# The second stage in 384-token units, with the second column halves of w1 and w2 decoded in place beside the last stage's first blocks

## The chip, the cores and the metric

One core of a Trainium2 chip runs the whole program in one launch. The metric is the device time of that launch in microseconds. TensorE (PE in the profile) multiplies matrices; VectorE (DVE), ScalarE (ACT) and GpSimd (POOL) do the elementwise work; every DMA is issued from the queue of SyncE (SP).

## The reference, cut to what matters

```python
x = attention_with_memory(q, k, v, M_prev, z_prev, beta)   # (4,8,576,64) -> 2304 x 512
h = x @ w_in                                               # 512 -> 2048
x = (h * tanh(softplus(h))) @ w_out                        # 2048 -> 512
a, b = x @ w1, x @ w2                                      # 512 -> 1024 each
out = (a * b @ w3) @ w_out2                                # 1024 -> 1024 -> 512
```

The weights arrive as 64-bit floats, so that each must be decoded on the chip from two 32-bit words. Matrix products are made from a rounded high part and a low part of each operand, three matmuls for one: high by high, high by low, low by high.

## The kernel before

**Stage one** is attention, pair of heads by pair of heads, up to about 257 us. Its result, x transposed, lies in two tiles `xt0` and `xt1` of 1152 tokens each.

**Stage two** (the loop over `u = (g, n)`, L597 to L618 of before) makes 24 units: four quarters `g` of the 2048 inner columns times six chunks `n` of 384 tokens. I number them 6g + n, from 0 to 23. A unit has 48 matmuls of 384 columns for h (`emit_h`, from `xt` and the quarter's weights `wqt`), the activation on ACT, a multiplication `y` on DVE (L436), the split into `gh` (ACT) and `gl` (DVE, L67), and 48 matmuls of 384 columns for x2 (`emit_x2`). The 48 go into four PSUM tiles `psX` out of a ring of three; DVE adds each to `x2` in SBUF (L532), so the fourth tile of a unit needs the first one's add to be over.

Beside the units run **decode steps**, of which one treats 128 rows of a weight matrix: an SP load into `draw`, six DVE instructions (L100, L101, L102, L104, L105, L106), and on POOL an add (L107), a rounding (L64) and a subtraction (L67 or L122). The `draw`, `da` and `de` tiles are rings of two in stage two. Two generators hand out steps of 512 columns: `load_quarter` makes the next quarter's `wqt` (eight steps), and `predecode` writes w1, w2 and w_out2 in two parts to DRAM (24 steps, two stores each), from where they are loaded later. The loop calls `steps(nextq, 2)` and `steps(pre, 1 if n < 4 else 2)` after each unit of the first three quarters.

In the last quarter the generator `fold` runs beside the units: 32 steps of 256 columns decode w3 (here POOL does the add alone), PE transposes them and multiplies them by w_out2, and the product goes through `wo` to DRAM. What is left of it runs on into the last stage. Then `wft` loads that product.

**Stage three** has blocks k of 512 tokens by 128 inner columns: `emit_ab(k)` makes 24 matmuls into two PSUM tiles from `x2h`/`room` (the split of x2, or `x2s` for every other span of tokens) and the weights `w12t`; ACT and DVE make the product and its split into a ring `room` of six; `emit_out(k)` multiplies it by `wft`, 12 matmuls, five blocks later. `w12t` has two slots: columns 0 to 511 of w1 and w2 serve blocks 0 to 3 of a span, columns 512 to 1023 blocks 4 to 7. The slots take the place of `xt0` and `xt1`; both are loaded from DRAM.

The order of instructions on each engine is fixed when the program is built: a scheduler takes the order of the code as priority and places by times that it assumes. Each engine then works strictly in that order.

Of the kernel before, what the change touches and what calls it, by code (L numbers as in the profile page):

```python
# [9 lines left out]
F32 = mybir.dt.float32  # L10
F32R = mybir.dt.float32r
# [10 lines left out]
def fused_kernel(ctx: ExitStack, tc, q, k, v, M_prev, z_prev, beta, w_in, w_out, w1, w2, w3, w_out2, out):  # L22
    nc = tc.nc
    B, H, S, D = q.shape
    NT, DM = out.shape
    FF = w_in.shape[1]
    FF2 = w1.shape[1]
    NP = H // 2
    NB = 5
    KD = DM // 128  # L30
# [10 lines left out]
    dram = ctx.enter_context(tc.tile_pool(name="dram", bufs=1, space=bass.MemoryType.DRAM))  # L41
# [9 lines left out]
    def psX():  # L51
        return bank("X")
# [4 lines left out]
    def f(ap):  # L57
        return ap.bitcast(F32)
# [22 lines left out]
    WN = 512  # L81
# [28 lines left out]
    def words(w, r0, c0):  # L110
        return w[r0:r0 + 128, c0:c0 + dec["w"]].bitcast(I32)

    def split_w(hi, lo, src):
        a, _ = decode(src)
        pool_round(hi, a)
        sub(lo, a, hi, nc.gpsimd)

    def split_to_dram(dst, src):

        a, e = decode(src)  # L120
        pool_round(e.bitcast(F32R), a)
        nc.gpsimd.tensor_tensor(out=a.bitcast(F32R), in0=a, in1=e, op=ALU.subtract)  # L122
        dm(out=dst[0], in_=e)
        dm(out=dst[1], in_=a)
# [9 lines left out]
    nc.vector.memset(half, 0.5)  # L134

    w_dram = dram.tile([2, FF2, DM], F32, name="w_dram")
    w1_dram = dram.tile([2, DM, FF2], F32, name="w1_dram")
    o2_dram = dram.tile([2, FF2, DM], F32, name="o2_dram")
    w2_dram = dram.tile([2, DM, FF2], F32, name="w2_dram")

    def predecode():
        for w, wd in ((w1, w1_dram), (w2, w2_dram), (w_out2, o2_dram)):
            for c in range(w.shape[0] // 128):
                for h in range(w.shape[1] // WN):
                    split_to_dram(wd[:, 128 * c:128 * c + 128, WN * h:WN * h + WN], words(w, 128 * c, WN * h))
                    yield

    xl = {}
# [10 lines left out]
    def load_quarter(g):  # L159
# [24 lines left out]
        out=mask, in_=mask, pattern=[[-1, 512]], compare_op=ALU.is_ge,  # L184
# [272 lines left out]
    pre = predecode()  # L457
# [54 lines left out]
    fk = ExitStack()  # L512
    fpool = [None]

    def emit_x2(u, beside):
        g, n = u
        t = wts[g]
        gg = gt.pop(u)
        c0 = CH * n
        for m in range(KD):  # L520
            o = psX()[:, 0:CH]
            ms = slice(128 * m, 128 * m + 128)
            for kk in range(KQ):
                gh, gl = (x[:, kk % 2] for x in gg[kk // 2])
                mm(o, t[:, 0, KD + kk, ms], gh, kk == 0, False)
                mm(o, t[:, 1, KD + kk, ms], gh, False, False)
                mm(o, t[:, 0, KD + kk, ms], gl, False, kk == KQ - 1)
            d = x2[:, m, c0:c0 + CH]
            if g == 0:
                r = nc.vector.tensor_copy(out=d, in_=o)  # L530
            else:
                r = nc.vector.tensor_tensor(out=d, in0=d, in1=o, op=ALU.add)  # L532
            steps(beside, 1)
        return r.ins
# [44 lines left out]
            held = piece  # L579
            yield  # L580

    def from_dram(t, d, cols):
        for i in range(2):
            dm(out=f(t[:, i]), in_=d[i, :, cols].rearrange("(k p) f -> p k f", p=128))

    def w_slot(s):
        t = xp.tile([128, 2, 2, KD, 512], F32R, tag=f"xs{s}", name="w12t", padded_shape=[128, 2, 2, KD, S])
        for i, wd in enumerate((w1_dram, w2_dram)):
            from_dram(t[:, i], wd, slice(512 * s, 512 * s + 512))
        w1t[s], w2t[s] = t[:, 0], t[:, 1]  # L590

    folding = fold()
    pre0 = iter(())
    nextq = iter(())
    prev = None
    w1t, w2t = [None, None], [None, None]
    for u in [(g, n) for g in range(NQ) for n in range(NCH)]:  # L597
        g, n = u
        last = g == NQ - 1
        if u not in gt:  # L600
            if last and fpool[0] is None:
                steps(nextq, 100)
                steps(pre, 100)
                dk.close()
                fpool[0] = fk.enter_context(tc.tile_pool(name="fp", bufs=1))
                decoder(fk, 3, 2, 256)
            y = emit_h(u, folding if last and n > 0 else iter(()))
        if last and n == 3:
            w_slot(0)
        if prev is not None:  # L610
            with tc.issue_after(emit_x2(prev, folding if last and n > 0 else pre0)):
                split_y(u, y)
        if not last:
            if n == 0:
                nextq = load_quarter(g + 1)
            steps(nextq, 2)
            steps(pre, 1 if n < 4 else 2)
        prev = u  # L618
    NM = FF2 // 128

    steps(folding, 100)
    fk.close()
    late = ctx.enter_context(tc.tile_pool(name="late", bufs=1))
    x2s = late.tile([128, 2, KD, 512], F32R, name="x2s")
    wft = wq.tile([128, 2, NM, DM], F32R, tag="wq0", name="wft")
    for s in range(2):
# [12 lines left out]
    wp3 = ctx.enter_context(tc.tile_pool(name="wp3", bufs=1, side="right"))  # L639
    T = 512  # L640
    RING = 6

    room = w2q[0].tile([128, 2 * RING + KD, T], F32R, tag="wq1", name="room")
    ring = room[:, 0:2 * RING].rearrange("p (r i) t -> p r i t", i=2)

    xs_ = {0: (wp3.tile([128, KD, T], F32R, name="x2h"), room[:, 2 * RING:]), 1: (x2s[:, 0], x2s[:, 1])}

    spans = [(t, min(T, NT - t)) for t in range(0, NT, T)]
    work = [(c, m) for c in range(len(spans)) for m in range(NM)]
# [10 lines left out]
    def emit_ab(k):  # L660
        c, m = work[k]
        n = spans[c][1]
        x = xs_[c % 2]
        pb, pa = (bank(t)[:, 0:n] for t in ("AA", "AF")[m % 2])
        m2 = slice(128 * (m % 4), 128 * (m % 4) + 128)
        for o, w in ((pb, w2t[m // 4]), (pa, w1t[m // 4])):
            for kk in range(KD):
                mm(o, w[:, 0, kk, m2], x[0][:, kk, 0:n], kk == 0, False)
                mm(o, w[:, 0, kk, m2], x[1][:, kk, 0:n], False, False)
                mm(o, w[:, 1, kk, m2], x[0][:, kk, 0:n], False, kk == KD - 1)  # L670
        t = ring[:, k % RING]
# [65 lines left out]
```

## Time and profile before

| | before |
|---|---|
| median of three runs | 1072.71 us (1072.01 to 1073.34) |
| the profiled execution | 1074.7 us |
| its span in the trace | 1072.9 us |
| PE busy | 1032.2 us, 96% |
| DVE, ACT, POOL busy | 667.9, 498.8, 348.1 us |
| mean granted TensorE clock | 0.984 |

A busy PE may run at the lower one of its two clock levels (1.2 instead of 2.4 GHz); the granted clock, 1.00 for the upper level throughout, tells that apart. Times in the trace count from the start of the span.

### The profile page before, as it was taken

What the parts mean: (1) busy time and instruction counts of PE and PEld (TensorE: products, weight loads), DVE (VectorE), ACT (ScalarE), POOL (GpSimd) and SP (SyncE); (2) the same over time, 40 slices, a digit from 0 to 9 for tenths busy, and PEclk for the clock granted to TensorE, in tenths of its full rate; (3) what the DMA queues carried; (4) which work ended last, traced back from release to release, by engine and by line L of the source; (5) the groups of instructions that cost most, each with busy time, mean ns of one, the idle gap of its engine ahead of it and who ended that gap; (6) DMA issues with size and microseconds to landing.
All of it is one profiled execution on the core that took longest, in us unless ns stands there. A gap on an engine that the chain in (4) does not pass through costs nothing.

```text
span 1072.9 us, 15339 instructions
## 1 busy us (share of the span) xinstructions
PE 1032.2 (96%) x5552; PEld 859.0 (80%) x5552; DVE 667.9 (62%) x1484; ACT 498.8 (46%) x1024; POOL 348.1 (32%) x361
## 2 busy tenths in 40 slices
PE   7999999999999998899989999999999999999998
PEld 4565665566899998898989999999768888888897
DVE  5999998754779779988879666667643112121111
ACT  4777777776545554455454554553232122211212
POOL 6767667522345536544455311111100000000000
PEclk9999999999999999899998999999989999999999
DMA  6434344310232422333223256226231010100101
GB/s 149 115 93 111 92 104 107 94 26 18 74 106 99 138 99 100 128 107 137 79 99 118 89 188 226 69 79 229 66 128 69 1 40 1 40 1 0 40 1 59
DMA packets 103675, 94.33 MB, mean 88 GB/s; under 512 B 69552, under 2 KB 75696, under 8 KB 103600
## 3 DMA queue, kind: packets, MB, share of 16 engines
q1 hardware_dynamic: 103600, 93.35, 28.0%
q8 instruction: 44, 0.72, 0.3%
q14 instruction: 31, 0.25, 0.1%
HBM read 71.83 MB, written 21.50 MB: 87 GB/s over the span
## 4 chain that ended last, share of the span: by engine, by line
PE 64%; DVE 17%; POOL 6%; issue 6%; DMA 4%; ACT 2%; SPq 1%; POOLq 0%; DVEq 0%; ACTq 0%
PE psA L61 25%; PE psX L61 20%; PE psF L61 11%; PE psF L378 5%; PE psX L259 3%; POOL da L107 3%; DVE da L104 2%; DVE gl L67 2%; DVE da L100 2%; DVE de L106 2%; DVE da L101 2%; DVE de L105 1%; DVE y L436 1%; DVE da L102 1%; POOL da L122 1%
## 5 line engine op out<-in xcount | busy, mean ns | idle before, releaser
L61 PE MATMUL psX<-gh,wqt 128*128 128x384 f32 x768 | 204.4, 347 | 18.2 <-DVE x L532 17.6
L107 POOL TENSOR_TENSOR da<-da,de 128x512 f32<-128x512 f32 (+1 forms) x88 | 107.4, 1222 | 320.6 <-DVE de L106 272.1
L61 PEld LDWEIGHTS psX<-gh,wqt 128*128 128x128 f32 x768 | 144.1, 195 | 22.1 <-DVE x L532 19.9
L61 PE MATMUL psX<-gl,wqt 128*128 128x384 f32 x384 | 132.9, 348 | 3.0 <-DVE gl L67 2.9
L61 PE MATMUL psA<-xt,wqt 128*128 128x384 f32 x624 | 118.2, 340 | 2.9 <-DVE y L436 2.9
L61 PEld LDWEIGHTS psA<-xt,wqt 128*128 128x128 f32 x624 | 110.4, 191 | 5.4 <-DVE y L436 3.9
L330 ACT ACTIVATE s<-s,acc 128x384 f32<-128x384 f32 (+3 forms) x144 | 84.9, 594 | 35.6 <-DVE acc L325 21.4
L100 DVE TENSOR_SCALAR da<-draw 128x512 int32<-128x512 int32 (+1 forms) x88 | 45.7, 523 | 80.5 <-PE psF L557 26.4
L444 ACT CAST gh<-y 128x768 fp32r<-128x768 f32 x48 | 40.1, 836 | 111.5 <-DVE y L436 69.4
L61 PE MATMUL psX<-wft,room 128*128 128x512 f32 x336 | 82.4, 390 | 0.0
L61 PE MATMUL psA<-x2h,w12t 128*128 128x512 f32 (+1 forms) x288 | 80.0, 354 | 0.0
L61 PEld LDWEIGHTS psX<-gl,wqt 128*128 128x128 f32 x384 | 75.3, 196 | 5.6 <-DVE gl L67 5.0
L325 DVE CUSTOM_DVE_ANT_0 s<-psA,mask 128x512 f32<-128x512 f32 (+2 forms) x144 | 65.0, 477 | 21.7 <-PE psA L61 19.1
L673 ACT COPY bs<-psA 128x512 f32<-128x512 f32 (+1 forms) x40 | 21.8, 546 | 116.5 <-PE psA L61 112.4
L61 PE MATMUL psX<-pt,raw 128*64 128x64 f32 (+4 forms) x576 | 75.0, 328 | 0.0
L61 PE MATMUL psF<-xt,wqt 128*128 128x384 f32 x408 | 74.7, 337 | 0.0
L61 PE MATMUL psA<-kt,qt 64*128 64x384 f32 (+3 forms) x256 | 71.3, 487 | 2.9 <-DVE acc L325 2.4
L61 PEld LDWEIGHTS psX<-wft,room 128*128 128x128 f32 x336 | 62.6, 188 | 12.7
L61 PEld LDWEIGHTS psF<-xt,wqt 128*128 128x128 f32 x408 | 71.9, 190 | 0.1
L380 ACT COPY pt<-psF 128x512 f32<-128x512 f32 (+1 forms) x112 | 58.9, 544 | 27.5 <-PE psF L378 23.6
L674 DVE TENSOR_TENSOR bs<-bs,psA 128x512 f32<-128x512 f32 (+1 forms) x20 | 12.7, 634 | 93.1 <-PE psA L61 92.4
L61 PE MATMUL psA<-x2s,w12t 128*128 128x512 f32 x288 | 67.9, 389 | 0.0
(114 smaller groups left out, 2036.6 us busy)
## 6 DMA issues: line engine op xcount, KB each, us to landing
draw<-in_moe_w_out_dram SPq DMA_DIRECT2D x24, 512.0 KB, 3.5
draw<-in_moe_w_in_dram SPq DMA_DIRECT2D x16, 512.0 KB, 3.9
draw<-in_moe_w_dram SPq DMA_DIRECT2D x16, 512.0 KB, 3.8
draw<-in_moe_w_dram SPq DMA_DIRECT2D x32, 256.0 KB, 3.0
w12t<-w_dram SPq DMA_DIRECT2D x8, 1024.0 KB, 9.0
out_dram<-ob SPq DMA_DIRECT2D x18, 256.0 KB, 2.0
raw<-in_q_dram SPq DMA_DIRECT2D x32, 128.0 KB, 2.7
raw<-in_k_dram SPq DMA_DIRECT2D x32, 128.0 KB, 3.1
```

The costliest lines, as they stand in the source:

```text
L61: nc.tensor.matmul(o, lhsT=l, rhs=r, start=start, stop=stop)
L67: return (eng or nc.vector).tensor_tensor(out=dst, in0=src, in1=f(hi), op=ALU.subtract)
L100: V.tensor_scalar(out=ai, in0=hw, scalar1=0x7FFFFFFF, scalar2=None, op0=ALU.bitwise_and)
L101: V.tensor_scalar(out=a, in0=a, scalar1=2.0 ** -15, scalar2=122879.9921875, op0=ALU.max, op1=ALU.min)
L107: nc.gpsimd.tensor_tensor(out=a, in0=a, in1=e, op=ALU.add)
L259: nc.tensor.transpose(pt[:, x:x + 128], src[:, i].rearrange("p h d -> p (h d)"), ident)
L325: nc.vector.tensor_tensor_reduce(out=s, in0=o, in1=m, op0=ALU.add, op1=ALU.min, scale=-scale, scalar=init, accum_out=a,)
L330: nc.scalar.activation(out=s, in_=s, func=AF.Exp, scale=-1.0, bias=a, accum_out=r)
L378: nc.tensor.transpose(o[:, 128 * x:128 * x + 128], src[:, 128 * jb:128 * jb + 128], ident)
L380: nc.scalar.copy(out=t[:, 0:n], in_=o[:, 0:n])
L444: nc.scalar.copy(out=gh, in_=y[i])
L673: nc.scalar.copy(out=bs, in_=pb)
```

## The change

`predecode` decodes only columns 0 to 511 of w1 and w2, and w_out2 first: 16 steps of 512 columns instead of 24. The loop's counts are made anew: `nextq` gives 2, 2, 1, 1, 1, 1 steps over a quarter, `pre` one step in units 1, 3, 4, 5 of a quarter and in unit 2 of the first two. The second halves are decoded by a new generator `second_half`, 16 steps of 256 columns, whose POOL instructions write straight into slot 1 of `w12t`. It is asked for steps in the last `emit_x2` and in blocks 0 to 3 of stage three; the rest comes before block 4. The decode pool stays open until then, and `x2s`, which takes its room, is allocated after.

```diff
     def predecode():
-        for w, wd in ((w1, w1_dram), (w2, w2_dram), (w_out2, o2_dram)):
+        for w, wd in ((w_out2, o2_dram), (w1, w1_dram), (w2, w2_dram)):
             for c in range(w.shape[0] // 128):
-                for h in range(w.shape[1] // WN):
-                    split_to_dram(wd[:, 128 * c:128 * c + 128, WN * h:WN * h + WN], words(w, 128 * c, WN * h))
+                split_to_dram(wd[:, 128 * c:128 * c + 128, 0:WN], words(w, 128 * c, 0))
+                yield
+
+    def second_half(t):
+        for h in range(2):
+            cs = slice(256 * h, 256 * h + 256)
+            for i, w in enumerate((w1, w2)):
+                for c in range(KD):
+                    split_w(t[:, i, 0, c, cs], t[:, i, 1, c, cs], words(w, 128 * c, WN + 256 * h))
                     yield
...
     def w_slot(s):
         t = xp.tile([128, 2, 2, KD, 512], F32R, tag=f"xs{s}", name="w12t", padded_shape=[128, 2, 2, KD, S])
-        for i, wd in enumerate((w1_dram, w2_dram)):
-            from_dram(t[:, i], wd, slice(512 * s, 512 * s + 512))
+        if s == 0:
+            for i, wd in enumerate((w1_dram, w2_dram)):
+                from_dram(t[:, i], wd)
...
-            steps(nextq, 2)
-            steps(pre, 1 if n < 4 else 2)
+            steps(nextq, 2 if n < 2 else 1)
+            steps(pre, 1 if n in (1, 3, 4, 5) or (g < 2 and n == 2) else 0)
...
     steps(folding, 100)
-    fk.close()
-    late = ctx.enter_context(tc.tile_pool(name="late", bufs=1))
-    x2s = late.tile([128, 2, KD, 512], F32R, name="x2s")
...
-    emit_x2(prev, pre0)
-    w_slot(1)
+    rest = second_half(w_slot(1))
+    emit_x2(prev, rest)
...
     for k, (c, m) in enumerate(work):
+        if k == 4:
+            steps(rest, 100)
+            fk.close()
+            late = ctx.enter_context(tc.tile_pool(name="late", bufs=1))
+            x2s = late.tile([128, 2, KD, 512], F32R, name="x2s")
+            xs_[1] = x2s[:, 0], x2s[:, 1]
         emit_ab(k)
+        if k < 4:
+            steps(rest, 3)
```

What the scheduler makes of it is seen at three places. The first is DVE in the second quarter, from the end of one unit to the adds of the next (`x_3429` is x2). Before, in unit 8 (L532 is the add):

```order
L104 SCALAR_TENSOR_TENSOR da<-draw,da 128x512
L100 TENSOR_SCALAR da<-draw 128x512
L105 TENSOR_SCALAR de<-da 128x512
L101 TENSOR_SCALAR da<-da 128x512
L106 SCALAR_TENSOR_TENSOR de<-draw,de 128x512
L102 TENSOR_SCALAR da<-da 128x512
L104 SCALAR_TENSOR_TENSOR da<-draw,da 128x512
L105 TENSOR_SCALAR de<-da 128x512
L106 SCALAR_TENSOR_TENSOR de<-draw,de 128x512
L100 TENSOR_SCALAR da<-draw 128x512
L101 TENSOR_SCALAR da<-da 128x512
L102 TENSOR_SCALAR da<-da 128x512
```

The next row there is the add. After, in unit 9 (L539 is the add):

```order
L67 TENSOR_TENSOR gl<-y,gh 128x768
L106 SCALAR_TENSOR_TENSOR de<-draw,de 128x512
L105 TENSOR_SCALAR de<-da 128x512
L106 SCALAR_TENSOR_TENSOR de<-draw,de 128x512
L539 TENSOR_TENSOR x_3429<-x_3429,psX 128x384
L100 TENSOR_SCALAR da<-draw 128x512
L443 TENSOR_TENSOR y<-y,psA 128x384 x2
```

Twelve decode instructions stood ahead of the first add, and three stand there now. The second place is POOL from the last step of 512 columns on. Before, to the end of its work:

```order
L107 TENSOR_TENSOR da<-da,de 128x512
L64 TENSOR_SCALAR de<-da 128x512
L122 TENSOR_TENSOR da<-da,de 128x512
L107 TENSOR_TENSOR da<-da,de 128x256 x32
L732 UNCONDITIONAL_BRANCH
```

After, the same place:

```order
L122 TENSOR_TENSOR da<-da,de 128x512
L107 TENSOR_TENSOR da<-da,de 128x256 x33
L64 TENSOR_SCALAR w12t<-da 128x256
L67 TENSOR_TENSOR w12t<-da,w12t 128x256
L107 TENSOR_TENSOR da<-da,de 128x256
L64 TENSOR_SCALAR w12t<-da 128x256
L67 TENSOR_TENSOR w12t<-da,w12t 128x256
```

The 16 new steps all stand behind the fold's 32. The third place is PE behind the fold's last matmul, where the second `psF` tiles of blocks 1 and 3 come first. Before, behind them:

```order
L61 MATMUL psF<-x2h,w12t 128x512
L61 MATMUL psX<-wft,room 128x512 x3
L61 MATMUL psA<-x2h,w12t 128x512
L61 MATMUL psA<-room,w12t 128x512
L61 MATMUL psA<-x2h,w12t 128x512 x2
```

After, the same place:

```order
L61 MATMUL psF<-x2h,w12t 128x512
L61 MATMUL psX<-wft,room 128x512 x27
L61 MATMUL psF<-x2h,w12t 128x512
L61 MATMUL psF<-room,w12t 128x512
L61 MATMUL psF<-x2h,w12t 128x512 x2
```

The output matmuls of blocks 0 to 2 were drawn ahead of block 4, and with them one tile of block 5 (its w1 part). Up to `psA` of block 3 PE's order in the last quarter and the fold is unchanged. Block 8, the first on `x2s`, stands behind 96 matmuls of blocks 4 to 7 and 72 of outputs 0 to 5, counted from the first output.

## Rows read from the trace of the kernel before

**Rows 1.** The page: busy time of each engine.

```profile
PE 1032.2 (96%) x5552; PEld 859.0 (80%) x5552; DVE 667.9 (62%) x1484; ACT 498.8 (46%) x1024; POOL 348.1 (32%) x361
```

**Rows 2.** Stretches: length, busy PE, PEld, DVE, ACT, POOL, granted clock, DMA, GB/s.

```profile
300.00:390.00 90.00, 86.22 (x479) 83.89 (x477) 72.90 (x119) 47.40 (x65) 42.16 (x37) 0.98 0.34 114
390.00:480.00 90.00, 80.45 (x422) 79.39 (x423) 84.98 (x130) 42.01 (x57) 47.16 (x39) 0.92 0.30 103
480.00:570.00 90.00, 80.20 (x435) 78.93 (x435) 74.41 (x122) 44.73 (x62) 44.59 (x36) 0.95 0.31 109
570.00:610.00 40.00, 40.00 (x232) 40.00 (x231) 30.14 (x55) 19.44 (x27) 19.04 (x15) 0.99 0.29 99
...
770.00:796.00 26.00, 21.88 (x87) 16.41 (x86) 12.28 (x34) 4.81 (x11) 2.92 (x4) 0.87 0.28 95
796.00:834.00 38.00, 38.00 (x169) 31.49 (x168) 14.20 (x22) 12.11 (x21) 0.00 (x0) 1.00 0.23 80
```

**Rows 3.** PE's longest wait in total, and two of its seven, in time.

```profile
PE psX L61 <- DVE x L532: 17.6, 7, 6.0
...
409.75 0.80 PE L61 MATMUL psX<-gh,wqt 128*128 128x384 f32 x2 [3.71 <-DVE x L532]
...
564.87 1.01 PE L61 MATMUL psX<-gh,wqt 128*128 128x384 f32 x2 [5.99 <-DVE x L532]
```

**Rows 4.** DVE, then POOL, ahead of the first of these waits, in time.

```profile
403.32 1.50 DVE L100 TENSOR_SCALAR da<-draw 128x512 int32<-128x512 int32 x1 [1.20 <-POOL wqt L67]
404.85 0.72 DVE L101 TENSOR_SCALAR da<-da 128x512 f32<-128x512 f32 x1
405.61 1.37 DVE L102 TENSOR_SCALAR da<-da 128x512 int32<-128x512 int32 x1
407.01 0.69 DVE L104 SCALAR_TENSOR_TENSOR da<-draw,da 128x512 int32<-128x512 int32 x1
407.74 0.43 DVE L105 TENSOR_SCALAR de<-da 128x512 int32<-128x512 int32 x1
408.20 0.69 DVE L106 SCALAR_TENSOR_TENSOR de<-draw,de 128x512 f32<-128x512 uint32 x1
...
409.14 0.55 DVE L532 TENSOR_TENSOR x<-x,psX 128x384 f32<-128x384 f32 x1
...
403.23 1.30 POOL L107 TENSOR_TENSOR da<-da,de 128x512 f32<-128x512 f32 x1
404.62 0.68 POOL L64 TENSOR_SCALAR wqt<-da 128x512 fp32r<-128x512 f32 x1
405.38 1.32 POOL L67 TENSOR_TENSOR wqt<-da,wqt 128x512 fp32r<-128x512 f32 x1
```

**Rows 5.** Timeline: the last of the fold's steps of 256 columns.

```profile
780.63 0.28 DVE L105 TENSOR_SCALAR de<-da 128x256 int32<-128x256 int32 x1
780.95 0.43 DVE L106 SCALAR_TENSOR_TENSOR de<-draw,de 128x256 f32<-128x256 uint32 x1
...
781.54 0.73 POOL L107 TENSOR_TENSOR da<-da,de 128x256 f32<-128x256 f32 x1 [1.77 <-DVE de L106]
```

**Rows 6.** Timeline: PE and DVE around the fold's end and the first output.

```profile
779.56 1.19 PE L61 MATMUL psF<-o,w3h 128*128 128x512 f32 x2 [1.40 <-DVE w3l L67]
...
782.25 1.05 PE L61 MATMUL psF<-o,w3h 128*128 128x512 f32 x2
...
786.93 0.63 PE L61 MATMUL psF<-o,w3h 128*128 128x512 f32 x2
...
787.30 0.43 DVE L67 TENSOR_TENSOR w3l<-psF,w3h 128x256 fp32r<-128x256 f32 x1 [1.00 <-ACT w3h L559]
...
795.53 0.84 PE L61 MATMUL psX<-wft,room 128*128 128x512 f32 x3
...
796.03 0.69 DVE L67 TENSOR_TENSOR room<-bs,room 128x512 fp32r<-128x512 f32 x1 [0.69 <-ACT room L675]
```

**Rows 7.** The chain that ended last: one block's 24 matmuls in stage three.

```profile
809.29 5.44 PE psA L61 x24
```

More of the change, by code (lines that the diff above doesn't have):

```diff
@@ L136, in fused_kernel @@
     w_dram = dram.tile([2, FF2, DM], F32, name="w_dram")
-    w1_dram = dram.tile([2, DM, FF2], F32, name="w1_dram")
+    w1_dram = dram.tile([2, DM, WN], F32, name="w1_dram")
     o2_dram = dram.tile([2, FF2, DM], F32, name="o2_dram")
-    w2_dram = dram.tile([2, DM, FF2], F32, name="w2_dram")
+    w2_dram = dram.tile([2, DM, WN], F32, name="w2_dram")
     def predecode():
-        for w, wd in ((w1, w1_dram), (w2, w2_dram), (w_out2, o2_dram)):
+        for w, wd in ((w_out2, o2_dram), (w1, w1_dram), (w2, w2_dram)):
             for c in range(w.shape[0] // 128):
-                for h in range(w.shape[1] // WN):
-                    split_to_dram(wd[:, 128 * c:128 * c + 128, WN * h:WN * h + WN], words(w, 128 * c, WN * h))
+                split_to_dram(wd[:, 128 * c:128 * c + 128, 0:WN], words(w, 128 * c, 0))
[6 more added lines that the diff above has]
+                    split_w(t[:, i, 0, c, cs], t[:, i, 1, c, cs], words(w, 128 * c, WN + 256 * h))
                     yield
@@ L580, in fold, with from_dram @@
             yield
-    def from_dram(t, d, cols):
+    def from_dram(t, d):
         for i in range(2):
-            dm(out=f(t[:, i]), in_=d[i, :, cols].rearrange("(k p) f -> p k f", p=128))
+            dm(out=f(t[:, i]), in_=d[i].rearrange("(k p) f -> p k f", p=128))
     def w_slot(s):
         t = xp.tile([128, 2, 2, KD, 512], F32R, tag=f"xs{s}", name="w12t", padded_shape=[128, 2, 2, KD, S])
-        for i, wd in enumerate((w1_dram, w2_dram)):
-            from_dram(t[:, i], wd, slice(512 * s, 512 * s + 512))
+        if s == 0:
+            for i, wd in enumerate((w1_dram, w2_dram)):
+                from_dram(t[:, i], wd)
         w1t[s], w2t[s] = t[:, 0], t[:, 1]
+        return t
     folding = fold()
@@ L644, in fused_kernel @@
     ring = room[:, 0:2 * RING].rearrange("p (r i) t -> p r i t", i=2)
-    xs_ = {0: (wp3.tile([128, KD, T], F32R, name="x2h"), room[:, 2 * RING:]), 1: (x2s[:, 0], x2s[:, 1])}
+    xs_ = {0: (wp3.tile([128, KD, T], F32R, name="x2h"), room[:, 2 * RING:])}
     spans = [(t, min(T, NT - t)) for t in range(0, NT, T)]
```

## The prediction

> **What bounds the kernel now.** I read the page's busy times first: PE is busy 96% of the span [rows 1], so a change can win only where PE stands still or runs at its lower clock. The table by stretches says where that is [rows 2]. From 300 to 610 us, the body of stage two, PE stands still for 3.8, 9.5, 9.8 and 0 us in the four stretches; the granted clock, 0.98, 0.92, 0.95 and 0.99, takes a further 1.8, 7.2, 4.5 and 0.4 us off its speed (a hundredth less is a hundredth of the stretch). Together 37.0 us, of which 31.0 lie between 390 and 570. From 796 to 834, in the last stage, PE is busy throughout at the full clock and POOL does nothing. The waits say why stage two loses: PE's longest wait is the fourth x2 tile's for the add of the first, 17.6 us in seven waits [rows 3]. The timeline ahead of one of them shows the add at 409.14 behind decode instructions: from 403.32 to 408.89 DVE works off one step, and only then one more instruction and the add [rows 4]. So in this stretch DVE's queue, not PE, sets the pace, and each wait of about 2 us or more is followed by a few us of PE at the lower clock: behind the fold's wait at 779.56 two matmuls of 512 columns take 1.05 us where they take 0.63 later [rows 6].
>
> The same rows price a step. While POOL works on its three instructions (403.23 to 406.70), DVE gets three of its own through, each ending about 0.3 us behind the end of one of POOL's: L100 at 404.82 behind 404.53, L101 at 405.57 behind 405.30, L102 at 406.98 behind 406.70. The other three then take 0.69, 0.43 and 0.69 us with POOL idle. The add, which reads PSUM, is not held up like this.
>
> **Stage two, part by part.** I count, in the order of DVE, the steps that end between the last adds of neighbouring units. Before, units 1 to 16 have 2 2 2 2 2, then 4 3 3 3 2 3 2 2 4, then 2 2: 40. After, they have 2 2 2 2 1, then 2 2 2 2 2 2 3 4 2, then 2 1: 33. The middle nine are about the stretch from 390 to 570 (the add at 409.14 is unit 6's first). The other seven units, all of two steps, lost 37.0 - 31.0 = 6.0 us, 0.86 a unit. At that rate the nine would lose 7.7 without their eight steps beyond two; they lost 31.0, so those eight cost 23.3 us, 2.9 each. After the change fourteen units have two steps or more (14 x 0.86 = 12.0) and three steps are beyond two, in units 12 and 13 (3 x 2.9 = 8.7); the two units of one step I put at nothing. That leaves 20.7 of 37.0: **16 us saved**. Ends: by the plain mean, 37.0/40 a step, the seven fewer save 6.5; the most is all 37. I stay at 16, nearest to the stretch where the steps in excess are taken away; what speaks for more is that only three decode instructions stand ahead of the adds in units 8 to 11, where ten or more stood. Units 17 and later have a full PE already, so a step fewer there is worth nothing; that PE is the cover, and 0 it stays. The two stores a step, sixteen fewer, and the four loads of slot 1, 1 MB each, are off SP's queue; they hid beside PE, and I take nothing for them.
>
> **Last stage.** PE's order up to block 3 is the same, so the fold's end stays as it is, earlier by what stage two saves; for the sum I keep the old times. The new steps cannot start early: on POOL they stand behind the fold's 32 adds, the last at 781.54 [rows 5], and on DVE the first step's last two instructions stand behind the fold's last low part, 787.30 to 787.73 [rows 6]. They add 0.28 and 0.43 us [rows 5], so POOL's first new add starts at about 788.6.
>
> What a step of 256 columns with three POOL instructions costs no row shows, since the fold has only the add. From below: POOL alone, the add's 0.73 [rows 5] and by the ratio 0.73/1.30 = 0.56 of 0.68 and 1.32 [rows 4], 0.38 and 0.74, with 0.1 us between them 2.1 us. From above: DVE and POOL wholly one behind the other, 3 x 0.28 + 0.28 + 2 x 0.43 = 2.0 and 1.85, 3.8 us. Between them: the step at 403.32, 5.57 us, scaled by 0.56 (POOL) to 0.65 (L105 at 0.28/0.43), 3.1 to 3.6. I take 3.1, since a fourth DVE instruction can pass before POOL's next add.
>
> Fifteen steps at 3.1 and the last one's 2.1 on POOL end at 788.6 + 46.5 + 2.1 = 837.2. In between stand ten DVE instructions of blocks 1 to 5, 0.69 us each [rows 6]; half of them I let POOL cover, 3.5 us. The last draws stand behind the second half of wft on SP, 2 MB: 2 us. So the decode ends at about 842.7. Behind it is the split for `x2s`, which waits until the pool is free, one ACT and one DVE instruction ahead of PE: 1.5 us, 844.2.
>
> When does PE want it? It starts outputs at 795.53 [rows 6], and has 96 + 72 matmuls ahead of block 8, at 5.44/24 = 0.227 us [rows 7] 38.1 us, so at 833.6. In that order it waits 10.6 us in all, piece by piece, since k = 4 to 7 take the tiles as POOL hands them over; queued behind a waiting matmul on PE are the outputs of blocks 4 and 5, too, and nothing else of PE's can be drawn forward. Behind a wait PE's clock is low, as at the fold's end, where 0.87 over 26 us costs 3.4 us [rows 2]; half of it I add, 1.7, since most of such a stretch falls into waiting here. **12 us given back.** The ends: a cycle of 2.1 us ends the decode at 788.6 + 31.5 + 2.1 + 7 = 829, and nothing is lost but the 1.5 to 2 us of `x2s`; 3.8 us ends it, with `x2s`, at 854.5, 21 us late, 24 with the clock.
>
> **Sum.** The profiled execution has 1074.7 us, of which 1.8 lie outside the span of 1072.9; less 16, plus 12, it is 1070.7. The median of the runs is 2.0 lower, 1072.71, so 1068.7; I say **1068.5 us**. A measurement of this kernel can tell about 0.2%, 2.1 us, from no change: faster is below 1070.6, slower above 1074.9.
>
> **Rivals.** (1) *The decode hides, and stage two gives more.* With a cycle near 2.1 us and stage two down to PE's pace: 25 saved (between 16 and 37), 2 given back, 1049.7. For it speaks that DVE is busy only 14.2 of 38 us from 796 to 834 and POOL not at all [rows 2]; against it, the pairs in rows 4. (2) *Slower: the new chain binds.* DVE and POOL take turns on every instruction of the 16 steps, 3.8 us each: 24 given back, 16 saved, 1080.7. It decides from where the chain is 14.3 us late (16 with the clock), at a cycle of (847.9 - 1.5 - 5.5 - 2.1 - 788.6)/15 = 3.3 us, just above mine. For it: L100, L101 and L102 all end behind a POOL instruction, and two of the three are more than twice as long as L105. Against it: one of DVE's instructions passes per POOL instruction without making that longer than 1.32 us.
>
> The Trainium skill has a rule for this, in "SBUF — State Buffer", section "Who interferes with whom": one port pair is shared by VectorE and GpSimd as an exclusive lock, held for a whole instruction, by VectorE instructions with two SBUF inputs or in a two-port mode. The trace agrees in kind: L101 ends 0.27 us behind POOL's L64, and the PSUM-reading add keeps its 0.55 us beside POOL's add. By a strict reading the rival's 3.8 us holds and the time is its 1080.7; by the measured step it is mine.
>
> (3) *Stage two hardly gains*, 6.5 us, since the wait for y and gl behind the same steps remains, and the chain costs 12: 1078.2.
>
> **How the numbers follow.** Mine 0.42, its own range 1060 to 1077, as its terms may be off by some 8; rival 1 0.25, rival 2 0.20, rival 3 0.13. Faster: rival 1 and 0.30 of mine, 0.55. Same: 0.09 of mine and 0.05 of rivals 2 and 3, 0.14. Slower: the rest, 0.31. The range of eight in ten leaves out half of rival 1 beyond 1049.7 and the worst of rival 2: 1050 to 1083.
>
> **What would show it.** PE's total wait for L539 adds falls from 17.6 to some 8 us, the rest of it in units 12 and 13, with the granted clock of the middle stretch up from 0.92. POOL, empty after 782 before, works for 48 to 57 us past the fold's end; PE waits some 10 us for POOL's `w12t` in that time, and its granted clock there falls below 1.00. If PE waits for POOL under 3 us, rival 1 holds; over 18, rival 2; if the L539 waits stay above 14 us, rival 3. I am wrong altogether if the fold's end itself moves.

## The result, and the profile after

The changed kernel takes **1061.89 us** (1060.50 to 1063.80) against 1073.03 us for the kernel before, run beside it: a ratio of 0.990, 95% interval 0.988 to 0.992. The prediction was 1068.5 us, in a range of 1050 to 1083. The direction was right, the size was not: 11 us faster, not 4.

The profiled execution took 1060.5 us, its span is 1058.4 us. It is the fastest of its kernel's four, and that of the kernel before, 1074.7 us, lies above its kernel's median: the traces differ by some 14 us where the medians differ by 11. PE's busy line falls by 10.2 us, DVE's by 6.5 [rows 1]:

```profile
PE 1022.0 (97%) x5552; PEld 850.4 (80%) x5552; DVE 661.4 (62%) x1532; ACT 499.4 (47%) x1024; POOL 350.4 (33%) x385
```

The stretches of stage two, then two of the last stage; the columns are those of [rows 2]:

```profile
300.00:390.00 90.00, 87.21 (x498) 85.93 (x498) 71.86 (x124) 51.46 (x70) 43.74 (x34) 1.00 0.28 94
390.00:480.00 90.00, 90.00 (x521) 90.00 (x520) 66.36 (x123) 51.20 (x71) 36.38 (x35) 1.00 0.27 90
480.00:570.00 90.00, 81.25 (x455) 79.97 (x454) 73.48 (x118) 44.27 (x61) 44.29 (x36) 0.98 0.27 95
570.00:590.00 20.00, 20.00 (x117) 20.00 (x116) 8.34 (x21) 11.72 (x17) 1.49 (x2) 1.00 0.09 27
762.00:790.00 28.00, 25.90 (x108) 21.00 (x107) 22.77 (x53) 3.69 (x7) 15.87 (x24) 0.94 0.70 241
790.00:822.00 32.00, 25.09 (x101) 19.66 (x100) 28.44 (x57) 8.25 (x15) 16.58 (x25) 0.95 0.14 45
```

From 390 to 480 us PE stands still for none of the time, at the full clock, where it lost 9.5 us and 0.92 of its clock before [rows 2]. From 300 to 390 it idles 2.8 us, from 480 to 570 8.75, with 1.8 us of clock (0.02 of 90): stage two still loses 13.3 us of its 37.0. In the last two stretches DVE is busy for 51.2 of 60 us and POOL for 32.5.

PE's longest wait in stage two, that for the add (L539 now, L532 before [rows 3]): total, times, longest.

```profile
PE psX L61 <- DVE x L539: 8.7, 4, 3.8
```

Two of the four, the first and the last, in time:

```profile
503.25 0.62 PE L61 MATMUL psX<-gh,wqt 128*128 128x384 f32 x2 [3.79 <-DVE x L539]
...
560.60 0.62 PE L61 MATMUL psX<-gh,wqt 128*128 128x384 f32 x2 [2.46 <-DVE x L539]
```

They are in units 12 to 15, 3.79, 1.29, 1.20 and 2.46 us. The other 2.7 us are unit 1's, at 310 (for gl) and 317.5 (for y). Units 2 to 11 show no wait.

To see where the time went I cut the program at the first matmul that stage three makes behind the fold, block 1's second tile. Before:

```profile
789.01 0.39 PE L61 MATMUL psF<-x2h,w12t 128*128 128x512 f32 x1
```

After, with the first matmul on `x2s`, block 8's:

```profile
762.45 0.39 PE L61 MATMUL psF<-x2h,w12t 128*128 128x512 f32 x1
...
819.20 1.19 PE L61 MATMUL psA<-x2s,w12t 128*128 128x512 f32 x4 [2.38 <-ACT bs L679]
```

Up to the cut 26.6 us are saved. From it to the end of the span it took 1072.9 - 789.0 = 283.9 us, and takes 1058.4 - 762.45 = 295.9: **12.0 us given back**.

### The profile page after: what moved, and what is told of

Same layout as the page of the kernel before. It is cut to its first block, busy times and chain, and to the rows that moved or that the text cites. A ratio compares the mean times of both kernels' runs of the same rounds, so it can differ in the third digit from the quotient of the medians.

```text
span 1058.4 us, 15388 instructions
## 1 busy us (share of the span) xinstructions
PE 1022.0 (97%) x5552; PEld 850.4 (80%) x5552; DVE 661.4 (62%) x1532; ACT 499.4 (47%) x1024; POOL 350.4 (33%) x385
## 4 chain that ended last, share of the span: by engine, by line
PE 66%; DVE 17%; POOL 7%; DMA 4%; issue 3%; ACT 2%; SPq 1%; POOLq 0%; DVEq 0%; ACTq 0%
PE psA L61 25%; PE psX L61 24%; PE psF L61 10%; PE psF L385 5%; PE psX L266 3%; POOL da L107 3%; DVE da L104 2%; DVE da L100 2%; DVE de L106 2%; DVE da L101 2%; DVE y L443 2%; DVE da L102 2%; DMA draw<-in_moe_w_dram 2%; DVE de L105 2%; DVE gl L67 1%
## 5 line engine op out<-in xcount | busy, mean ns | idle before, releaser
L61 PE MATMUL psX<-gh,wqt 128*128 128x384 f32 x768 | 197.3, 336 | 8.9 <-DVE x L539 8.7
L61 PEld LDWEIGHTS psX<-gh,wqt 128*128 128x128 f32 x768 | 138.8, 188 | 12.0 <-DVE x L539 10.0
L61 PE MATMUL psX<-gl,wqt 128*128 128x384 f32 x384 | 128.4, 336 | 0.9 <-DVE gl L67 0.9
L100 DVE TENSOR_SCALAR da<-draw 128x512 int32<-128x512 int32 (+1 forms) x96 | 43.2, 454 | 94.9 <-PE psF L564 28.6
L61 PEld LDWEIGHTS psX<-gl,wqt 128*128 128x128 f32 x384 | 72.2, 188 | 2.1 <-DVE gl L67 1.5
L385 PE MATMUL psF<-ident,s 128*128 128x128 f32 x400 | 65.4, 282 | 1.2 <-ACT pt L387 1.2
```

Source lines behind the costliest of these rows:

```text
L61: nc.tensor.matmul(o, lhsT=l, rhs=r, start=start, stop=stop)
L100: V.tensor_scalar(out=ai, in0=hw, scalar1=0x7FFFFFFF, scalar2=None, op0=ALU.bitwise_and)
L385: nc.tensor.transpose(o[:, 128 * x:128 * x + 128], src[:, 128 * jb:128 * jb + 128], ident)
```

## Experiments

**The two halves apart.** `e1_no_second` keeps the new stage two and leaves out the decode of the second halves: slot 1 is filled from DRAM, from the first halves; `e4_chain_alone` keeps the old stage two and adds the new decode.

`e1_no_second`, against the changed kernel:

```diff
-        if s == 0:
-            for i, wd in enumerate((w1_dram, w2_dram)):
-                from_dram(t[:, i], wd)
+        for i, wd in enumerate((w1_dram, w2_dram)):
+            from_dram(t[:, i], wd)
...
-    rest = second_half(w_slot(1))
+    rest = iter(())
     emit_x2(prev, rest)
+    w_slot(1)
```

`e4_chain_alone`, against the kernel before (`second_half`, `w_slot` and `x2s` as in the change):

```diff
+    rest = second_half(w_slot(1))
+    emit_x2(prev, rest)
...
+        if k < 4:
+            steps(rest, 3)
```

> The changed kernel with its stage two as it is, but without the decode of the second halves: slot 1 of the weights is loaded from DRAM as before, from the first halves, so that decode is the part of the computation that is left out. It shows what stage two saves by itself. Theory (stage two saves about 26 us, by the fold's end at 762.45 instead of 789.01, and the decode chain in the last stage gives about 12 back): 1047 to 1051 us, and PE waits for nothing but the fold between 762 and 820. Rival (the chain costs little by itself, and the last stage is longer for another reason, such as PE's new order of outputs): 1056 to 1062 us.

> The kernel before with its whole stage two (24 steps of predecode, old order and counts) and the changed last stage on top: slot 1 is decoded in place, and the second halves in DRAM stay unused. It shows the last stage's part by itself. Theory: the chain gives back 12 us, 1083 to 1088. Rival (the chain costs only because stage two now ends earlier): 1073 to 1078.

Measured: `e1_no_second` 1048.12 us, ratio 0.977 (0.975 to 0.978), 25 us below the kernel before. `e4_chain_alone` 1087.25 us, ratio 1.013 (1.011 to 1.015), 14 above it. The sum, -25 + 14 = -11, is what the change measures, so the halves add up. The cut says the same: in `e1_no_second` it stands at 762.06 and 283.9 us follow, as before the change; in `e4_chain_alone` it stands at 788.13 and 297.9 follow. What PE waits for in `e4_chain_alone` from 780 on:

```profile
PE psX L61 <- ACT room L682: 4.1, 1, 4.1
PE psA L61 <- ACT bs L680: 2.4, 1, 2.4
PE psF L61 <- DVE bs L681: 2.1, 1, 2.1
```

The same three waits stand in the changed kernel's tail (4.2, 2.4 and 2.1 us); `e1_no_second` has the last kind alone, 0.8 us.

**The number of steps or their place.** The change made the steps fewer and put them elsewhere. `e2_spread` leaves the kernel before its 24 steps of `predecode` and spreads the counts; `e3_old_counts` gives the changed kernel, with its 16, the old counts back.

`e2_spread`, against the kernel before:

```diff
-            steps(nextq, 2)
-            steps(pre, 1 if n < 4 else 2)
+            steps(nextq, 2 if n < 2 else 1)
+            steps(pre, 1 if n < 2 else (2 if n == 3 or n == 5 else 1))
```

`e3_old_counts`, against the changed kernel:

```diff
-            steps(nextq, 2 if n < 2 else 1)
-            steps(pre, 1 if n in (1, 3, 4, 5) or (g < 2 and n == 2) else 0)
+            steps(nextq, 2)
+            steps(pre, 1 if n < 4 else 2)
```

> The kernel before with all its 24 steps of predecode, only the counts of the loop are spread: nextq 2, 2, 1, 1, 1, 1 and pre 1, 1, 1, 2, 1, 2 over a quarter. Theory A (the number of steps in a unit beyond two costs, by DVE's total load): the same 40 steps, so no more than 5 us from before, 1068 to 1075. Theory B (what costs is decode instructions bunched ahead of the x2 adds, and the spread alone undoes that): 1050 to 1060.

> The changed kernel with the counts of before in the loop (nextq 2 a unit, pre 1 or 2): the eight steps fewer stay, the spread is undone, and the steps crowd in quarters 0 and 1. Theory A (load): steps beyond two remain in the first two quarters, about six of them, and quarter 2 has a full PE: 1062 to 1068. Theory B (bunching): the stalls come back in full, 1070 to 1076.

Measured: `e2_spread` 1073.06 us, ratio 0.999 (0.998 to 1.001); `e3_old_counts` 1078.4 us, ratio 1.005 (1.003 to 1.006). In `e3_old_counts` DVE's order has 2 2 2 2 2 4 3 3 3 3 0 2 3 1 steps in units 1 to 14 and none in 15 and 16, and PE's longest wait and the stretch from 390 to 480 us look like the kernel before [rows 2, 3] and not like the changed one:

```profile
PE psX L61 <- DVE x L539: 16.5, 6, 5.2
```

```profile
390.00:480.00 90.00, 79.01 (x429) 77.93 (x430) 85.29 (x131) 42.23 (x59) 47.15 (x39) 0.94 0.31 106
```

So with eight steps fewer, but crowded, stage two keeps most of its loss; the cut comes at 780.11, 17.7 us later than with the same steps spread. `e2_spread` shows the other side: its order has three steps in units 8, 11, 15 and 17 and two in the others from 1 to 18, and it loses some 21 us from 300 to 610, not 37. Two steps a unit are not free there: units 2, 3, 6, 7, 12 and 13, with two each, wait 2.1, 2.2, 1.3, 0.7, 1.4 and 3.7 us. The last of these:

```profile
533.75 0.61 PE L61 MATMUL psX<-gh,wqt 128*128 128x384 f32 x2 [3.72 <-DVE x L532]
```

What it gains it loses again behind 610 us. Its steps reach into units 17 and 18; from 610 to 640 PE stands still for 4.7 us (0.9 before) and its clock is 0.89 (1.00 before), and from 740 to 788 it loses 7 us more than before, wait and clock together. The cut comes at 788.14, 0.9 us earlier than before. Its stretches from 570 on, PE nearly full in the first and not in the second:

```profile
570.00:610.00 40.00, 39.63 (x227) 38.99 (x226) 29.68 (x59) 21.52 (x29) 16.67 (x15) 1.00 0.33 108
610.00:640.00 30.00, 25.28 (x131) 24.32 (x130) 21.93 (x39) 11.29 (x19) 12.79 (x11) 0.89 0.64 218
```

Spread alone and fewer steps alone each gained nothing; the change has both.

**Fewer still, and half the chain.** `e5_fewer_still` is `e1_no_second` with the decode of w2's first half left out too (four steps fewer; w1's first half stands in for it); `e6_half_chain` decodes w1's second half in stage two (four steps more) and leaves only w2's to the last stage.

`e5_fewer_still`, against `e1_no_second`:

```diff
-        for w, wd in ((w_out2, o2_dram), (w1, w1_dram), (w2, w2_dram)):
+        for w, wd in ((w_out2, o2_dram), (w1, w1_dram)):
...
-            steps(pre, 1 if n in (1, 3, 4, 5) or (g < 2 and n == 2) else 0)
+            steps(pre, 1 if n in (1, 3, 5) or (g == 2 and n == 4) else 0)
```

`e6_half_chain`, against the changed kernel:

```diff
+        for w, wd, c0 in ((w_out2, o2_dram, 0), (w1, w1_dram, 0), (w2, w2_dram, 0), (w1, w1b_dram, WN)):
...
-            for i, w in enumerate((w1, w2)):
+            for i, w in ((1, w2),):
...
+            steps(pre, 1)
```

> The kernel of e1_no_second with four more steps taken out of stage two: w2's first half is not decoded either, and both weights' slots are loaded from w1's first half, so that the decode of w2 is left out. In DVE's order units 1 to 17 now have 2 2 2 1 0, 2 2 3 3 1 0, 2 2 3 3 0 0 steps, four beyond two. Theory (units of two steps lose nothing behind a light unit; only crowded ones lose, some 3 us a step beyond two): stage two loses as much as in e1_no_second, whose waits these would be, only elsewhere: 1045 to 1050 us. Rival (each step costs by DVE's total load, some 3 us): 1034 to 1040 us.

> The changed kernel with w1's second half decoded in stage two again (four more steps of 512 columns, one pre step after every unit), so that only w2's eight steps of 256 columns are left for the last stage. Theory (crowding; units 1 to 17 have 2 2 3 2 1, 2 2 3 2 2 2, 3 2 3 2 2 1): stage two loses 0 to 5 us more than in the changed kernel, and the decode chain, half as long, ends ahead of PE's need, so that 8 to 12 us are won: 1050 to 1057 us. Rival (load: four steps at 2.9 us): 1060 to 1065 us.

Measured: `e5_fewer_still` 1062.65 us, ratio 0.990 (0.988 to 0.991), 14.5 us **slower** than `e1_no_second`, which has four steps more. Its order has 2 2 2 1 0 2 2 3 3 1 0 2 2 3 3 in units 1 to 15, gaps and pairs of threes, and waits again in the stretch that was full:

```profile
390.00:480.00 90.00, 84.47 (x479) 83.83 (x478) 69.93 (x116) 47.74 (x65) 38.81 (x33) 0.98 0.25 83
```

Its total wait for L539 adds is 13.6 us. Unit 3, with two steps, waits 2.9 us there. A price by the number of steps, in all or in a unit, does not fit this run. `e6_half_chain` took 1068.48 us, ratio 0.995 (0.994 to 0.997). From its cut, 778.44, 286.8 us follow: half the chain gives back 2.9 us, not half of 12. The four steps more cost 16 us of stage two, much more than was expected of them; its order has a three in units 3, 8, 12 and 14 and one step in 17.

**The chain in the last stage.** `e7_own_ring` starts the second halves earlier, in buffers of their own (128 columns, one `draw`, two `da` and `de`); `e8_round_on_act` moves the chain's rounding from POOL to ACT.

`e7_own_ring`, against the changed kernel:

```diff
-                decoder(fk, 3, 2, 256)
+                decoder(fk, 2, 2, 256)
+                own_ring.update(pool=fk.enter_context(tc.tile_pool(name="dec2", bufs=1)), raw=1, n=2, w=128)
...
+        if last and n == 5:
+            rest = second_half(w_slot(1))
```

`e8_round_on_act`, against the changed kernel:

```diff
-                    split_w(t[:, i, 0, c, cs], t[:, i, 1, c, cs], words(w, 128 * c, WN + 256 * h))
+                    a, _ = decode(words(w, 128 * c, WN + 256 * h))
+                    nc.scalar.copy(out=t[:, i, 0, c, cs], in_=a)
+                    sub(t[:, i, 1, c, cs], a, t[:, i, 0, c, cs], nc.gpsimd)
```

> The changed kernel with the second halves decoded out of rings of their own (128 columns a step, 32 steps, w2 ahead of w1; the fold's draw ring is two instead of three) and asked for right after the last unit's h, so that they no longer stand behind the fold's 32 adds on POOL. Theory (the 12 us are given back because the chain starts only when the fold is over): most of the chain lies beside the fold, 1048 to 1055 us. Rival (DVE has no room beside the fold, so that the fold's end moves out instead): 1060 to 1068 us.

> The changed kernel with the rounding of the second halves on ACT instead of POOL: POOL has two instructions a step, 0.41 us less. Theory (DVE and POOL, by turns, set the chain's pace of some 3.2 us a step): 0.3 to 0.5 us a step, so 4 to 8 us less: 1054 to 1058 us. Rival (the loads of draw or DVE alone set the pace): 1060 to 1063 us.

Measured: `e7_own_ring` 1103.66 us, ratio 1.028 (1.026 to 1.029), far outside what was expected. PE waits 26.6 us for POOL's `w12t`, 0.3 us in the changed kernel, and DVE for loads:

```profile
DVE da L100 <- DMA draw<-in_moe_w_dram: 65.5, 31, 4.1
```

Of these 31 waits 27 are the chain's, with its one `draw`, and four the fold's, whose ring has one `draw` less here; the cut moves out too, by 12.2 us to 774.67. The run changes both rings at once. It doesn't tell whether an earlier start in two `draw` buffers would pay; that was not tried. `e8_round_on_act` took 1062.52 us, ratio 0.989 (0.987 to 0.992), no change. POOL has an instruction of 0.41 us less a step, but waits 0.5 us for ACT in its place, and the last step ends at 815.62 us where it ended at 815.93:

```profile
810.28 0.74 POOL L107 TENSOR_TENSOR da<-da,de 128x256 f32<-128x256 f32 x1 [0.69 <-DVE de L106]
811.54 1.02 POOL L67 TENSOR_TENSOR w12t<-da,w12t 128x256 fp32r<-128x256 f32 x1 [0.52 <-ACT w12t L153]
```

So POOL's share of a step is no shorter, and the run doesn't tell which engine sets the chain's pace.

**Crowding moved about.** Left was what the changed kernel still loses in units 12 to 15, where its order has 3 4 2 2 steps. Two lines of counts move the crowding: `e9_second_quarter` has one three, in unit 7, and a last step in unit 17; `e10_third_quarter` has 3 3 2 2 1 from unit 12 on.

Both against the changed kernel, `e9_second_quarter` first:

```diff
-            steps(pre, 1 if n in (1, 3, 4, 5) or (g < 2 and n == 2) else 0)
+            steps(pre, (0,0,1,1,1,1)[n] if g ==1 else (0,1,1,1,1,1)[n])
```

```diff
-            steps(pre, 1 if n in (1, 3, 4, 5) or (g < 2 and n == 2) else 0)
+            steps(pre, 1 if n in ((1, 2, 3, 4, 5) if g < 2 else (2, 3, 4, 5)) else 0)
```

> The changed kernel with one other line of counts: predecode gives a step in units 2, 3, 4, 5 of the second quarter and in units 1 to 5 of the first and the third (a step in unit 1 of the second quarter goes to unit 2 of the third). Same steps in all, same output; DVE's order has 2 steps in each of units 1 to 16 but unit 5 and 11 (1) and unit 7 (3), and one in unit 17; the changed kernel has 3 and 4 in units 12 and 13 and none beyond 16. Theory (crowding: what is lost hangs on steps beyond two in a unit): the changed kernel's waits at 503 to 561 us (8.7 us with their lower clock some 10) nearly go, one three-step unit costs 2 to 3, and the fold's end comes 5 to 9 us earlier than 762.4: 1053 to 1057 us. Rival (the loss belongs to the end of the third quarter, where the first steps of the last quarter's weights and the last of predecode meet, whatever the count): the waits there stay, 1060 to 1063. A second rival is that the step in unit 17 shifts the fold's start, as in e2_spread, by 3 to 5 us: 1058 to 1060.

> The changed kernel with predecode giving a step in units 2, 3, 4, 5 of the third quarter where it gave 1, 3, 4, 5. Same steps in all, same output; DVE's order has 3 and 3 steps in units 12 and 13 (3 and 4 before), 2 in 14 and 15, 1 in 16. Theory (each step beyond two costs some 3 us): two steps beyond two where there were three, so 3 us off, 1058 to 1060 us, with the waits at 503 to 561 us down from 8.7 to some 6. Rival (the place, not the count): no change, 1060 to 1063.

Measured: 1062.38 us (ratio 0.990, 0.989 to 0.991) and 1062.01 us (0.990, 0.988 to 0.993). By the times alone my theory had fallen, since both stayed with the rival of the place. The trace of `e9_second_quarter` says otherwise: the stretch that lost 10.6 us is full, and a new wait has come at its end.

```profile
480.00:570.00 90.00, 90.00 (x521) 90.00 (x521) 63.83 (x113) 55.19 (x76) 38.86 (x35) 1.00 0.23 79
570.00:590.00 20.00, 16.00 (x90) 15.68 (x89) 9.78 (x23) 9.49 (x13) 4.67 (x4) 0.95 0.23 79
590.00:620.00 30.00, 30.00 (x158) 29.07 (x157) 20.67 (x53) 12.49 (x19) 4.47 (x6) 0.92 0.55 190
```

The timeline ahead of that wait tells why:

```profile
580.61 1.29 POOL L122 TENSOR_TENSOR da<-da,de 128x512 fp32r<-128x512 f32 x1
...
581.93 0.32 SPq L124 DMA_DIRECT2D w_dram<-da  x1
...
583.99 1.28 SPq L94 DMA_DIRECT2D draw<-in_moe_w_dram  x3
...
587.90 0.29 DVE L100 TENSOR_SCALAR da<-draw 128x256 int32<-128x256 int32 x1 [9.23 <-issue]
588.23 0.29 DVE L101 TENSOR_SCALAR da<-da 128x256 f32<-128x256 f32 x1
588.44 0.55 DVE L539 TENSOR_TENSOR x<-x,psX 128x384 f32<-128x384 f32 x1
...
589.04 1.01 PE L61 MATMUL psX<-gh,wqt 128*128 128x384 f32 x2 [4.00 <-DVE x L539]
```

The add at 588.44 stands behind the fold's first two instructions (256 columns). Their `draw` lies in the room of the old decode pool. POOL ends at 581.90, the store of the last step's low part is issued, 2.1 us later the fold's load, 3.9 us after that DVE goes on, having stood idle for 9.23 us. That the room is free only with that store is my reading; the trace shows the order and names no releaser. `e10_third_quarter` has the same wait in unit 16, where its last step stands, beside 4.7 us left in units 12 and 13:

```profile
576.60 0.29 DVE L100 TENSOR_SCALAR da<-draw 128x256 int32<-128x256 int32 x1 [10.06 <-issue]
...
577.74 0.77 PE L61 MATMUL psX<-gh,wqt 128*128 128x384 f32 x2 [3.08 <-DVE x L539]
```

So each of my two tables bought one loss with the other. Three earlier runs have this wait as well: `e3_old_counts` (2.4 us, in unit 14), `e5_fewer_still` (4.9) and `e6_half_chain` (2.9). Unit 14 isn't late, so a late unit isn't the condition. In all five DVE ends the last step of 512 columns behind the first add of a unit, 5 to 10 us ahead of the time when the next unit's add could run; in the changed kernel it ends at unit 15's first add (560.1 us), and unit 16's, at 573.4, keeps nobody waiting. It is the place of the second rival, by another mechanism: the fold's first product isn't later than in the changed kernel (606.58 for 607.12 us), PE waits inside the unit.

**Neither.** If that is so, a table with two steps in every unit and none after unit 15 should gain. The loop has no place for it, but stage one has: there, in the changed kernel, PE is busy for all of 180 to 260 us and DVE for 51.6 of these 80.

`e11_two_a_unit`, against the changed kernel; `e12_one_late` has 14 in place of 15, and one step more in the third quarter:

```diff
-        if 2 <= p < 12:
+        if 2 <= p < 15:
             steps(background, 1)
...
+            steps(pre, (0, 1, 1, 1, 1, 1, 0, 1, 1, 1, 1, 0, 0, 1, 1, 0, 0, 0)[6 * g + n])
```

> The changed kernel with three of its steps of predecode taken into stage one, which asks for a background step in pairs 12, 13 and 14 too, and the counts of the loop made to suit. Same steps in all, same output. DVE's order has two steps in every unit from 1 to 15 (one in 5), none beyond, so neither a third step in a unit nor a last step beside the change of the decode pool. Theory after e9 and e10 (a unit of two steps costs nothing; a third costs 2 to 3 us; and steps after unit 15 delay the change of pools, behind whose first load DVE holds back x2's add, 3 to 4 us and as much again at the lower clock): what stage two loses falls from 13 to about 3 us (the waits at 310 and 317 stay), 9 to 10 us off less 0 to 3 for the steps in stage one, where PE is busy throughout and DVE for 60%: 1052 to 1056 us. Rival (the work has to be done somewhere, and PE pays the same for it wherever it stands, as e9 and e10 look if only their times are read): 1060 to 1063.

> As e11_two_a_unit, with pairs 12 and 13 alone, so that one step more is left for the loop: DVE's order is the same up to unit 15, and has one step in unit 16. Same steps in all, same output. It tells the change of pools apart. Theory: the add in unit 16 or 17 waits behind the first instruction of the fold's first step, 3 to 4 us, with 1 to 3.5 us at the lower clock behind it: 4 to 7 us slower than e11_two_a_unit, 1057 to 1062. Rival (a single step in a unit hides): within 1.5 us of e11_two_a_unit.

Measured: `e11_two_a_unit` **1052.33 us** (1049.30 to 1052.77), ratio 0.980 (0.979 to 0.981), inside what was expected, and better than both kernels. Its stage two is full but for the first stretch:

```profile
300.00:390.00 90.00, 86.85 (x496) 85.26 (x495) 72.30 (x125) 51.05 (x70) 43.60 (x34) 1.00 0.28 95
...
480.00:570.00 90.00, 90.00 (x521) 90.00 (x520) 62.01 (x119) 52.16 (x73) 35.22 (x31) 1.00 0.22 73
570.00:590.00 20.00, 20.00 (x119) 19.97 (x118) 10.01 (x26) 10.89 (x16) 0.89 (x2) 1.00 0.01 2
```

It loses 3.2 us from 300 to 590, 2.7 of them in the waits of unit 1. Those stand 1.5 us later than in the changed kernel (319.0 for 317.5), the most that the three steps can have cost in stage one. The cut comes at 751.18, 11.3 us earlier: 13.3 - 3.2 - 1.5 = 8.6 of it are stage two's, and some 1.8 are the lower clock of the changed kernel's fold (0.92 from 740 to 762 us), which this profiled execution, 3 us below the median of its five, doesn't show; 0.9 stays open. `e12_one_late` took 1054.65 us, ratio 0.983 (0.981 to 0.984), 2.3 us more than `e11_two_a_unit`: one late step costs neither 4 to 7 us nor nothing. Its one wait of the new kind has the shape of that in `e9_second_quarter`:

```profile
566.12 0.29 DVE L100 TENSOR_SCALAR da<-draw 128x256 int32<-128x256 int32 x1 [6.81 <-DMA draw<-in_moe_w_dram]
...
569.01 0.55 DVE L539 TENSOR_TENSOR x<-x,psX 128x384 f32<-128x384 f32 x1
...
569.61 0.61 PE L61 MATMUL psX<-gh,wqt 128*128 128x384 f32 x2 [1.92 <-DVE x L539]
```

Here the last step makes weights that stay in SBUF, so no store stands ahead of the change of pools: the fold's load goes out at 562.55 us, as POOL's last instruction ends at 562.53. The clock stays at 1.00. The mechanism holds, its price is smaller than I said.

## Why the prediction was wrong in size

- **What bounds the kernel** was right: DVE's order in front of the x2 adds. `e3_old_counts` and `e5_fewer_still` show that fewer steps alone win nothing; what counts is their place. What I took for a sign of it was too simple: I read that ten or more decode instructions stood ahead of the adds of units 8 to 11 before (twelve, ten, nine and five did), and in the changed kernel twelve stand ahead of unit 6's first add, 8.5 us of work, without a wait, while twelve in unit 12, 10.7 us of work, cost 3.79 us. I also counted one step too many after: unit 16 has none, so units 1 to 16 have 32 steps, not 33; only the low end of the range of savings hangs on it.
- **The failed step is the price by the number of steps in a unit, above all the 0.86 us for every unit of two**, 12.0 of the 20.7 us that I left to stage two. I took it from seven units outside the middle, and spread their 6.0 us over them. Nine of the fourteen units that I charged, 2 to 4 and 6 to 11, have two steps each and lose nothing in the changed kernel: 7.7 us charged for 0, and the whole sum was 20.7 for a measured 13.3. Unit 1 loses 2.7 us at 310 and 317.5; every run has two steps in it, so whether they are the cause stays open. Two steps are not free in themselves either: in `e2_spread` and `e5_fewer_still` units with two wait, in `e11_two_a_unit` units 2 to 15, with two in all but unit 5, lose 0.3 us. What counts is where a step's instructions stand on DVE against `gl`, `y` and the adds; a rule that gives the wait from the order no run here shows.
- **The excess**: three steps at 2.9 us, 8.7, in units 12 and 13. Measured 8.7 us of waits and 1.8 of clock, in units 12 to 15. That the size came out is luck: units 12 and 13 wait 5.1 us, and the other 3.7 stand in units 14 and 15, which have two steps. The price isn't one of a step. The one three in `e9_second_quarter` cost 2.7 us of waits in units 7 to 10, the three in unit 9 of the kernel before none, and the end of the decode has a price of its own, as `e9_second_quarter` and `e12_one_late` show.
- **The fold**: the cut moved by 26.6 us, of which stage two's body explains 37.0 - 13.3 = 23.7. The fold itself, from its first product to the cut, takes 155.3 us for 156.8, so 1.5 us lie in it, and 1.4 us are left open.
- **The last stage** came out as worked out: 12.0 us given back for 12 in the traces, 14 by the times in `e4_chain_alone`. The chain on POOL ran from 761.94 to 815.93 us, 54.0 us; I had 788.6 to 842.7, 54.1. One of its cycles near the end, up to the next:

```profile
806.73 0.74 POOL L107 TENSOR_TENSOR da<-da,de 128x256 f32<-128x256 f32 x1 [1.15 <-DVE de L106]
807.56 0.41 POOL L64 TENSOR_SCALAR w12t<-da 128x256 fp32r<-128x256 f32 x1
808.04 0.74 POOL L67 TENSOR_TENSOR w12t<-da,w12t 128x256 fp32r<-128x256 f32 x1
809.93 0.74 POOL L107 TENSOR_TENSOR da<-da,de 128x256 f32<-128x256 f32 x1 [1.15 <-DVE de L106]
```

  A cycle is 3.2 us for the predicted 3.1. DVE in the same time:

```profile
806.89 0.73 DVE L101 TENSOR_SCALAR da<-da 128x256 f32<-128x256 f32 x1
807.65 0.45 DVE L102 TENSOR_SCALAR da<-da 128x256 int32<-128x256 int32 x1
808.14 0.92 DVE L104 SCALAR_TENSOR_TENSOR da<-draw,da 128x256 int32<-128x256 int32 x1
809.10 0.29 DVE L105 TENSOR_SCALAR de<-da 128x256 int32<-128x256 int32 x1
809.42 0.42 DVE L106 SCALAR_TENSOR_TENSOR de<-draw,de 128x256 f32<-128x256 uint32 x1
```

  L101, L102 and L104 each end 0.1 to 0.3 us behind one of POOL's three; L105 and L106 follow with POOL idle, and the next add waits for them. The Trainium skill ("SBUF — State Buffer", section "Who interferes with whom") has VectorE instructions with two SBUF inputs or in a two-port mode and GpSimd's exclude each other on a shared port pair. The trace agrees in kind: L105 and L106 are held too where they meet an instruction of POOL (0.70 us at 795.32 and 0.86 at 777.97, for 0.29 and 0.42 here). Even so the step isn't the 3.8 us of rival 2: in this cycle the instructions held under POOL's three add only the 0.28 us by which the last of them, L104, ends behind POOL.
- **What PE waits for in the last stage** I named wrongly in part, though the sum was right. I said that PE would wait for POOL's `w12t`; it does so for 0.3 us. It waits 4.2 us for ACT's rounding of a block's product, 2.4 for ACT's copy `bs`, 2.1 for DVE's product. The longest of them, at 797.98, goes back to a multiplication that stands on DVE behind the chain's own instructions, though its inputs were there from 794.18 on:

```profile
793.59 0.59 ACT L679 COPY bs<-psA 128x512 f32<-128x512 f32 x1 [18.03 <-PE psA L61]
...
796.39 0.29 DVE L100 TENSOR_SCALAR da<-draw 128x256 int32<-128x256 int32 x1
796.59 0.68 DVE L680 TENSOR_TENSOR bs<-bs,psA 128x512 f32<-128x512 f32 x1
797.30 0.62 ACT L681 CAST room<-bs 128x512 fp32r<-128x512 f32 x1 [3.12 <-DVE bs L680]
797.98 1.47 PE L61 MATMUL psX<-wft,room 128*128 128x512 f32 x3 [4.19 <-ACT room L681]
```

  It is the mechanism of stage two again. The 2.4 us are the wait for `x2s` that I had worked out: ACT splits `x2s` as POOL's last instruction ends, at 815.93, and its copy `bs` stands behind that.

```profile
815.96 2.18 ACT L663 CAST x2s<-x 128x512 fp32r<-128x512 f32 x4 [1.84 <-POOL w12t L67]
```

  So PE reaches block 8 only when the chain's end lets it, and what it waits earlier comes off that wait; this is my reading of why the sum held, and no run separates it. The sign that I had named, under 3 us of waiting for POOL's `w12t`, would have given the case to rival 1, and wrongly. The lower clock behind these waits, 0.94 and 0.95 over 60 us, takes 3.3 us more; I had 1.7.
- **The rivals**: the first was right in its first half (25 us saved), wrong in its second. The second needed a cycle of 3.3 us and got 3.2. The third had 17.6 us of waits fall to no less than 14; they fell to 8.7.

## What to carry to other kernels

Where side work is woven into the order of an engine that others wait for, look at where its pieces stand between two waits, not at the load or a count: here units of two steps waited for nothing in one order and up to 3.7 us in another, and four steps fewer in a worse place cost 14.5 us. A table that moves side work must also say what stands at its end: in `e9_second_quarter` the next phase's first load went out behind the last piece's store, and the first instruction of that phase held the engine for 9.2 us. When two tables give the same time, look at their traces before dropping the theory, since each may have paid another price.

## What the runs showed of the chip

The clock behind a wait is not a fixed price. The same waits of 1.4, 1.5 and 2.1 us at the fold's end were followed by a granted clock of 0.91 from 740 to 780 us in the changed kernel and in `e12_one_late`, and of 1.00 in `e11_two_a_unit`, whose profiled execution was the fastest of its five, 3 us below their median (length, busy PE, granted clock, DMA, GB/s):

```profile
740.00:760.00 20.00, 14.37 (x61) 1.00 0.64 194
760.00:780.00 20.00, 19.64 (x87) 1.00 0.62 213
```

The wait of 2.0 us in unit 1, at 317.5 us in the same order, left the clock from 300 to 390 at 1.00 in the changed kernel and at 0.98 in `e9_second_quarter` and `e10_third_quarter`. So the prediction's rule, that each wait of about 2 us or more is followed by the lower clock, doesn't hold. I had charged the clock by a share of each stretch; what decides whether it falls, no run here shows.
